# Splitting GpSimd's tensor instructions, and telling the planner of the port that GpSimd shares with VectorE

## The chip, the cores and the metric

The kernel runs on one core of one Trainium2 chip. The metric is the device time of one execution in microseconds (us). The engines are named as in the profile: PE (TensorE, matmul), PEld (its weight loads), DVE (VectorE), ACT (ScalarE), POOL (GpSimd) and SP (SyncE, which only issues DMAs).

## The reference

For each of 8 batches, cosine attention over 12 heads of 448 tokens and 64 channels; its output, laid out as 448 x 768, goes through a two-dimensional Fourier transform whose real part is added, a layer norm and a two-layer FFN with ReLU and a residual:

```python
q_n = q / (norm(q) + 1e-06); k_n = k / (norm(k) + 1e-06)
attn = softmax(q_n @ k_n.T / tau); x = attn @ v          # (8, 12, 448, 64) -> (8, 448, 768)
X = fft(fft(x, axis=1), axis=2); u = x + real(X)
un = (u - mean(u)) / sqrt(var(u) + 1e-06)
out = u + max(un @ w_ch1, 0) @ w_ch2                      # 768 -> 3072 -> 768
```

Inputs and output are float32; the kernel computes its matmuls in bf16.

## The kernel before

The kernel doesn't write out an order by hand. It records about 3,000 operations, each with a list of engines that may do it, an estimated duration, a priority, and what it reads and writes (`Plan.add`, L105). `Plan.schedule` (L143) then plays them through in time: whenever an engine is free it takes, among the operations that are ready first, the one with the lowest priority number. What comes out is one fixed order per engine. `Plan.emit` writes each engine's order with semaphore waits, so on the chip each engine works strictly in that order, and an operation that is late holds back all that is queued behind it on its engine. `SHIFT` (L28) adds constants to the priorities of named operations; it is a table of numbers and decides the order in detail.

Names follow one scheme, a step, its numbers, and the batch: `qk00_2` is a score matmul of batch 2, `sc0_3` a scaling for batch 3. The stages of a batch, and the engines that they use:

- Norms and transposes. For batches 2 to 7 SP loads 128 x 768 pieces of q and k (`ld_`), ACT squares (`sq`), DVE sums (`ss`), ACT and DVE make the reciprocal norm (`ln`, `nrm`, `eps`, `rcp`), POOL multiplies (`sc0` to `sc6`, L722) and SP transposes by DMA (`tr`). For batches 0 and 1 the scalings (`scK`, `scQ`, `scT`) are on DVE and the transposes on PE (`tk`, `tq`).
- Attention. `qk` on PE, `ex` on ACT (exp from PSUM), `pv` on PE, `rd` and `x` on DVE (normalisation), then `fa`, `f`, `g` on DVE, which fold the sequence for the transform.
- Transform. `fs` and `fd` on PE, then `pq`, `u` (residual), `bs`, `ba` (layer-norm statistics), `un` on DVE, and `tru`, a transposing DMA that SP issues and that gives PE its operand.
- FFN. `h` on PE is the first layer, `relu` on ACT or DVE takes it out of PSUM. PSUM has two banks for these products (pool M), so PE stands still when the ReLU two steps back isn't done. For batch 0 the second layer is done directly (`y`). From batch 1 on, two token tiles share seven products `m1` to `m7` in place of eight, which needs sums of hidden blocks (`s1` to `s4`, DVE, L1217) and four sums of weight blocks, `t1` to `t4`, in three parts each (`t10`, `t11`, `t12` and so on; L1276), made once. `t3` overwrites weights that batch 0 still reads, so `t3` and `t4` wait for batch 0's last product. `m6` needs `t2`, `m5` `t1`, `m7` `t3`, `m4` `t4`. Outputs leave PSUM by ACT and get a residual from POOL (`fa0p`, `fv0p`, `fm0p`; L1148), or by DVE (`fin`), and are stored by SP or by an indirect DMA from POOL (`sc_1_0`).

PE has the most work, so the planner fills it: PE's idle places in the plan get filler matmuls (`Plan.fill`, L243), whose results nobody reads. A filler is put in PE's order, waits for the DVE operation that the plan has finished just before it, and writes columns 450 to 512 of a PSUM bank. They keep PE from idling for long; the trace records a TensorE clock that is granted at full or at half rate.

POOL's DMAs (weights `W1_`, `W2_`; values `ld_v`) stand in POOL's order like its arithmetic. The W1 and W2 loads are chained: each waits for the landing of the third before it.

Of the kernel before, what the change touches and what calls it, by code (L numbers as in the profile page):

```python
# [2 lines left out]

# [3 lines left out]
AluOp = mybir.AluOpType  # L7
# [21 lines left out]
    "ix0": {0: 108.5}, "ldt0": {0: 220.8}, "scT0_0": {0: 4.6}, "scK1_0": {0: 211.1}, "ek1_0": {0: 171.4}, "ek2_0": {0: -26.8}, "tq2_0": {0:  # L29
    136.3}, "et0_0": {1: -181.4}, "ld_q1_0": {0: 5.1}, "sqK1_0": {0: 9.2}, "nrm0": {2: -2.9}, "eps0": {2: -104.2}, "ssT1_0": {0: -11.8}, "ln0":  # L30
    {3: -6.1}, "scT3_0": {0: -68.7}, "scK4_0": {0: -50.6}, "scQ4_0": {0: 6.1}, "scT4_0": {0: 72.4}, "scK5_0": {0: 18.9}, "scT5_0": {0: -38.2},
    "ek3_0": {0: 0.7}, "tq3_0": {0: -15.6}, "eq3_0": {0: -21.7}, "et1_0": {1: 112.3}, "half": {1: 331.9}, "ld_v2_0": {0: -9.9}, "pv11_0": {0:
    17.1}, "rd1_0": {0: 250.5}, "qk22_0": {0: -118.5}, "tpd": {0: 74}, "tqd": {0: 221.6}, "u0_0": {3: 2.3}, "u224_0": {0: 25.7}, "u1_0": {2:
    11.1, 4: 7.7}, "eu00_0": {0: -63.8}, "bs1_0": {0: -1.8, 1: -2.6}, "un2_0": {0: -44.8}, "W1_0": {0: 0.013}, "scK0_1": {0: -0.7}, "scT0_1":
    {0: -306.7}, "tq2_1": {0: -24.4}, "ln1": {2: -23.6}, "rcp1": {2: 63.5}, "sqQ1_1": {0: -27.7}, "scK5_1": {0: 644.3}, "scQ5_1": {0: 190.2},
    "ek3_1": {0: -9.4}, "tq4_1": {0: 5.7}, "eq4_1": {0: -135.4}, "tt1_1": {0: -229.4}, "ex0_1": {0: 7.5, 1: -623, 3: 418.3}, "pv00_1": {0: 127},
    "ex1_1": {2: 107.9}, "qk1t_1": {0: 20.1}, "ex3_1": {0: 509.1}, "qk2t_1": {0: 311.3}, "pv20_1": {0: 40.2}, "fa1_1": {1: -84.5}, "relu0_0":
    {0: 13.6}, "relu10_0": {0: 199.5}, "fin01_0": {0: 115.9}, "t40": {0: 144.2}, "t21": {0: 84.1}, "u0_1": {3: -26}, "u1_1": {3: 31.1, 4: 24.3,
    5: 52.7}, "bs0_1": {1: -82.5}, "bs3_1": {0: -0.6}, "sq0_2": {0: -193}, "ln2": {0: 5.2}, "sc1_2": {0: 53.9}, "ld_k0_2": {0: -1.8}, "ss3_2":
    {1: 7}, "eps2": {3: 52.6, 5: 52.6}, "ss5_2": {0: 25.7}, "sq5_2": {1: 343.5}, "ld_k2_2": {0: -6.2}, "ex3_2": {0: 306, 1: 306}, "g0_2": {0:  # L40
    33.7}, "te0_2": {0: 14.9}, "qk4t_2": {0: 250.7}, "x4_2": {0: 3.5}, "g1_2": {0: -470.2}, "s21_1": {0: 252.1}, "fd0_2": {0: 0.2}, "u0_2": {1:
    -300.3}, "pq1_2": {0: 46.9}, "un0_2": {0: 4.2}, "ss0_3": {0: -154.8}, "ss1_3": {1: -75.1}, "tr1_3": {0: 14.7}, "ss2_3": {0: 449.6}, "sq2_3":
    {1: -527.6}, "tr3_3": {0: 56.4}, "ss4_3": {1: -209.3}, "eps3": {4: 98.6}, "sq6_3": {0: 1.2}, "ss6_3": {1: -24.9}, "ex0_3": {3: 2}, "x0_3":
    {0: 41.1}, "ex1_3": {2: 103.4}, "qk20_3": {0: -294.6}, "pv50_3": {0: 69.4}, "rd4_3": {0: -2.5}, "f01_3": {0: 230.6}, "relu22_2": {0: 148.6},
    "fd1_3": {0: 116.4}, "u1_3": {3: 275.9, 4: 212.2}, "bs1_3": {0: 7.8}, "rs1_3": {0: 154.6}, "tr1_4": {0: -3.5}, "ss4_4": {0: -161.2},
    "ld_k2_4": {0: -0.1}, "qk20_4": {0: -3}, "pv20_4": {0: 84.3}, "pv50_4": {0: 78}, "gc1_4": {0: 152.1}, "relu20_3": {0: 11.7}, "s21_3": {0:
    37.2}, "s31_3": {1: 42.1}, "ln5": {2: -325.5}, "pv00_5": {0: 1.4}, "qk1t_5": {0: 2.3}, "qk20_5": {0: -436.1}, "pv30_5": {0: 1.5}, "fa0_5":
    {1: 325.8}, "g0_5": {0: 10.3}, "relu8_4": {1: 56.3}, "fd0_5": {0: 4.5}, "pq0_5": {0: 280.5}, "pq1_5": {1: 218.4}, "sq6_6": {0: 33.9},
    "rcp7": {0: -136.1}
}  # L50


# [3 lines left out]
class Op:  # L56
    __slots__ = ("engs", "eng", "fn", "durs", "prio", "deps", "raw", "start", "end",
                 "idx", "acquire", "uses", "dma", "name", "seq", "margin", "serve", "order")

    def __init__(self, engs, fn, durs, prio, name, serve=0.0, margin=0.0):  # L60
        self.engs = engs
        self.eng = None
        self.fn = fn
        self.durs = durs
        self.serve = serve
        self.prio = prio
        self.deps = set()
        self.order = ()
        self.raw = set()
        self.start = self.end = None  # L70
        self.idx = None
        self.acquire = None
        self.uses = ()
        self.dma = None
        self.name = name
        self.margin = margin

# [10 lines left out]
class Plan:  # L88
# [54 lines left out]
    def schedule(self):  # L143
# [6 lines left out]
        ready = {e: [] for e in self.ENGS}  # L150
        free = {"pe": 1.0, "act": 2.0, "dve": 1.0, "pool": 0.85, "sp": 0.7}
# [35 lines left out]
        while left:  # L187
# [38 lines left out]
            if e == "pool" and op.dma is not None and self.order[e] and self.order[e][-1].dma is None:  # L226
                d += 0.6
            op.start = t
# [14 lines left out]
    def fill(self, t0, t1, after, make, least=0.3):  # L243

        live = {0: [], 1: []}
        for op in self.ops:
            for t in op.acquire or ():
                if t.pool == "M":
                    live[t.slot].append((op.start, max(u.end for u in t.users), t))
        out, t = [], t0  # L250
        for op in self.order["pe"]:
            if op.start > t0 and op.end <= t1 + 1.0 and op.start - t > least:
                bank = [x for x in (0, 1) if not any(a < op.start and b > t for a, b, _ in live[x])]

                for x in range(int((op.start - t) / 0.4)) if bank else ():
                    at = t + 0.4 * x
                    new = Op(("pe",), make(bank[0], 8), (0.288,), 0, "warm")
                    new.eng, new.start, new.end = "pe", at, at + 0.288
                    new.deps.add(after)
                    new.deps.add([o for o in self.order["dve"] if o.end + PE_LAT <= at + 0.1][-1])  # L260
                    new.deps.update(u for a, b, tile in live[bank[0]] if b <= t for u in tile.users[-2:] if u.eng != "pe")
                    out.append(new)
            out.append(op)
            t = max(t, op.end)
# [77 lines left out]
class Kern:  # L342
# [336 lines left out]
    def norm(self, b):  # L679
        P = self.P  # L680
# [17 lines left out]
        for i, (kind, t, dmas) in enumerate(items):  # L698
# [15 lines left out]
            for x in range(ns):  # L714
# [7 lines left out]
            P.add(("pool",), lambda v, i=i, buf=buf, qh=qh: v.tensor_tensor(  # L722
                v3(qh), v3(buf), RN[:, i, :].unsqueeze(2).to_broadcast((128, H, DH)), AluOp.mult),
                (1.5,), pr, f"sc{i}_{b}", reads=bn + [f"RN_{i}t"],
# [415 lines left out]
    def fin(self, b, tile, op, ob, c, ut, src, nm):  # L1140
# [3 lines left out]
        if src == "a":  # L1144
# [3 lines left out]
            self.P.add("pool", lambda g: g.tensor_tensor(self.OUTB[:, ob, cs], self.OUTB[:, ob, cs], self.U[:, ut, cs], AluOp.add), 0.95, -1,  # L1148
                       f"{nm}p_{b}", reads=[on] + self.unames(b, ut), writes=[on])
# [112 lines left out]
    def sums(self, done):  # L1262
# [7 lines left out]
        for k in range(3):  # L1270
            for nm, o, a, bb, rd, wr, af in (
# [4 lines left out]
                P.add(("pool", "dve"), lambda e, o=o, a=a, bb=bb: e.tensor_tensor(o, a, bb, AluOp.subtract), (3.15, 1.8), 190, f"{nm}{k}",  # L1276
                      reads=rd, writes=wr + old * (nm != "t3"), after=af)
# [109 lines left out]
```

## Time and profile before

| | us |
|---|---|
| median of 3 runs | 603.44 (602.99 to 607.24) |
| the profiled execution | 601.36 |
| its span, first to last instruction | 599.5 |
| before the first FFN matmul (`h0_0`) | 52.7 |
| end of batch 0's last product | 122.7 |
| first FFN matmul of batch 1 (`h0_1`) | 130.05 |

The profile records one execution; its own time, 601.36 us, is 1.9 us above its span and 2.1 us below the median of the three runs. In its rows a group has a line of the kernel, an engine, an operation, what it writes and reads, and a count; then busy time, the mean duration of one, and the idle time before them with what ended it. The planner's names above are put to the trace's instructions by their place in each engine's order. In a timeline row the first number is the start from the span's beginning, the second the length.

### The profile page before, as it was taken

Reading aid. Unit: us, or ns where it says so; the run is one execution under the profiler, and the core shown is the slowest. Engines: PE = TensorE matmul, PEld = TensorE weight load, DVE = VectorE, ACT = ScalarE, POOL = GpSimd, SP = SyncE. Lnnn points to the kernel's source line nnn. Section 1 sums busy time; section 2 is a strip of 40 time slices with the busy share of each in tenths; the row PEclk is TensorE's granted clock in tenths of the full one; section 3 lists DMA queues with packets and bytes.
Section 4 is the critical chain, followed back from the end, with each engine's and each line's share of the span. In section 5 each row is a group of like instructions: output and inputs, shape, how many; then the busy total and the mean of one; then the engine's idle time right before and its main releaser. Section 6 shows DMA issues by size and latency. Waiting matters only on the chain.

```text
span 599.5 us, 15228 instructions
## 1 busy us (share of the span) xinstructions
PE 572.9 (96%) x6298; PEld 445.5 (74%) x6298; DVE 431.0 (72%) x969; ACT 353.6 (59%) x678; POOL 212.0 (35%) x214
## 2 busy tenths in 40 slices
PE   4888999988999999999999999999999999999997
PEld 4568786666778578678778678668878778678684
DVE  6868887899789868985768767986888477711313
ACT  7885796435876886348766786458536644224140
POOL 8843344568244144331270426222340120200302
PEclk9889999979999999999999999999999999999999
DMA  9999999945179459354299149654492010210001
GB/s 215 126 203 222 177 196 144 170 103 109 28 150 148 68 147 111 81 121 107 55 136 162 42 130 111 110 121 119 62 104 56 15 54 2 67 40 27 27 27 53
DMA packets 187637, 62.13 MB, mean 104 GB/s; under 512 B 166704, under 2 KB 185392, under 8 KB 187568
## 3 DMA queue, kind: packets, MB, share of 16 engines
q1 hardware_dynamic: 129648, 38.35, 33.2%
q0 software_dynamic: 57920, 22.81, 29.6%
q8 instruction: 49, 0.80, 0.6%
q14 instruction: 20, 0.16, 0.1%
HBM read 51.90 MB, written 11.01 MB: 105 GB/s over the span
## 4 chain that ended last, share of the span: by engine, by line
PE 82%; DVE 7%; POOL 5%; ACT 2%; DMA 2%; issue 2%; POOLq 0%; DVEq 0%
PE PS L1095 35%; PE PS L1126 30%; PE PS L838 5%; PE PS L801 4%; PE PS L925 2%; PE PS L963 2%; DVE U L991 2%; PE PS L832 2%; DMA W1b<-in_moe_w_ch_dram 1%; POOL TX L1276 1%; DVE ACG L1020 1%; DVE HQ L1217 1%; DMA W2b<-in_moe_w_ch_dram 1%; PE PS L813 1%; POOL W1b L512 1%
## 5 line engine op out<-in xcount | busy, mean ns | idle before, releaser
L1095 PE MATMUL PS<-UNT,W1b 128*128 128x256 bf16 (+1 forms) x2304 | 236.1, 260 | 3.5 <-DVE HQ L1111 2.5
L1095 PEld LDWEIGHTS PS<-UNT,W1b 128*128 128x128 bf16 x2304 | 199.0, 98 | 28.0 <-issue 3.2
L781 ACT ACTIVATE E<-PS 128x900 bf16<-128x900 f32 (+1 forms) x192 | 147.8, 829 | 27.8 <-PE PS L801 24.5
L1126 PE MATMUL PS<-W2b,HQ 128*128 128x384 bf16 x768 | 133.9, 326 | 0.0
L1111 ACT ACTIVATE HQ<-PS 128x512 bf16<-128x512 f32 x117 | 69.9, 597 | 92.1 <-PE PS L1095 91.5
L1126 PEld LDWEIGHTS PS<-W2b,HQ 128*128 128x128 bf16 x768 | 73.6, 98 | 46.6 <-issue 2.0
L1217 DVE TENSOR_TENSOR HQ<-HQ 128x512 bf16<-128x512 bf16 x141 | 70.2, 522 | 43.0 <-ACT HQ L1111 30.2
L722 POOL TENSOR_TENSOR QH<-STG,SM 128x768 bf16<-128x768 f32 x42 | 62.9, 1498 | 74.6 <-DVE SM L535 46.6
L1148 POOL TENSOR_TENSOR OUTB<-OUTB,U 128x384 f32<-128x384 f32 x33 | 32.0, 969 | 157.0 <-ACT OUTB L1146 156.7
L1126 PE MATMUL PS<-TX,HQ 128*128 128x384 bf16 x396 | 71.3, 326 | 0.0
L1126 PEld LDWEIGHTS PS<-TX,HQ 128*128 128x128 bf16 x396 | 37.7, 98 | 24.1 <-issue 1.3
L838 PE MATMUL PS<-VB,E 128*128 128x65 bf16 x1152 | 52.5, 195 | 0.0
L838 PEld LDWEIGHTS PS<-VB,E 128*128 128x128 bf16 x1152 | 49.0, 99 | 1.5
L715 ACT ACTIVATE QH<-STG 128x384 f32<-128x384 f32 x84 | 42.3, 523 | 13.1 <-DVE SM L717 9.8
L1111 DVE TENSOR_SCALAR HQ<-PS 128x512 bf16<-128x512 f32 x45 | 31.1, 690 | 26.0 <-PE PS L1095 25.7
L717 DVE TENSOR_REDUCE SM<-QH 128x6 f32<-128x384 f32 x84 | 43.7, 541 | 6.6 <-ACT QH L715 6.4
L1176 POOL DMA_INDIRECT out_dram<-OUTB,IDX x20 | 21.0, 1050 | 76.6 <-DVE OUTB L1154 43.8
L832 PE MATMUL PS<-VZ,E 128*128 128x130 bf16 x192 | 41.9, 221 | 2.1 <-DVE X L858 1.8
L801 PE MATMUL PS<-QT,KT 64*128 64x225 bf16 x576 | 40.2, 260 | 2.3 <-DVE SM L534 1.4
L991 DVE TENSOR_TENSOR U<-ACG,X 128x384 bf16<-128x384 f32 (+3 forms) x70 | 40.8, 611 | 0.8
L761 POOL DMA_DIRECT2D VB<-in_v_dram x24 | 25.6, 1073 | 27.2 <-PE PS L838 24.6
L801 PEld LDWEIGHTS PS<-QT,KT 64*128 64x128 bf16 x576 | 22.5, 94 | 17.1 <-issue 4.6
(135 smaller groups left out, 649.5 us busy)
## 6 DMA issues: line engine op xcount, KB each, us to landing
STG<-in_k_dram SPq DMA_DIRECT2D x18, 384.0 KB, 3.7
STG<-in_q_dram SPq DMA_DIRECT2D x18, 384.0 KB, 4.5
VB<-in_v_dram POOLq DMA_DIRECT2D x24, 192.0 KB, 7.5
W1b<-in_moe_w_ch_dram POOLq DMA_DIRECT2D x12, 384.0 KB, 7.7
W2b<-in_moe_w_ch_dram POOLq DMA_DIRECT2D x12, 384.0 KB, 6.5
out_dram<-OUTB SPq DMA_DIRECT2D x7, 384.0 KB
TX<-in_k_dram SPq DMA_DIRECT2D x2, 576.0 KB, 5.5
TX<-in_q_dram SPq DMA_DIRECT2D x2, 576.0 KB, 6.0
```

Of the source, the lines that this page charges most:

```text
L715: P.add("act", lambda a, sq=sq, src=buf[:, w * x:w * x + w]: a.activation(sq, src, ACTF.Square), t_act(w), pr, f"sq{i}_{b}", reads=bn, wri ...
L717: P.add("dve", lambda v, o=SS[:, i, H // ns * x:H // ns * (x + 1)], sq=sq: v.tensor_reduce(o, sq.rearrange("p (h d) -> p h d", d=DH), AX.X ...
L722: P.add(("pool",), lambda v, i=i, buf=buf, qh=qh: v.tensor_tensor(v3(qh), v3(buf), RN[:, i, :].unsqueeze(2).to_broadcast((128, H, DH)), Al ...
L781: return a.activation(o, self.PS[:, bk:bk + nc_, 0:SQ2], ACTF.Exp, scale=1.0 / self.tau)
L801: i = pe.matmul(self.PS[:, bk + h, c0:c0 + NK], self.KT[r, jj, kt * 128:(kt + 1) * 128], self.QT[r, jj, cols], start=True, stop=True)
L832: r = pe.matmul(o, st(6), self.VZ[:, j, :], start=not split, stop=(split and i == 0), skip_group_check=True)
L838: r = pe.matmul(o[:, 65 * h:65 * h + 65], st(2 * kt + h), self.VB[:, kt, 2 * j + h, :], start=(split and i == h == kt == 0), stop=((not sp ...
L991: return v.tensor_tensor(U[o0:o0 + n, ut, cs].rearrange("p (i e) -> p i e", e=2), src, X[i0:i0 + n, x, cs].rearrange("p (i e) -> p i e", e ...
L1095: r = pe.matmul(self.PS[:, bk, x * n:(x + 1) * n], self.W1b[:, j, ft * 128:(ft + 1) * 128], self.UNT[:, j, cs], start=(j == 0), stop=(j == ...
L1111: return e.activation(o, i, ACTF.Relu) if e is self.nc.scalar else e.tensor_relu(o, i)
L1126: r = pe.matmul(self.PS[:, bk, 0:n], lhs(f), rhs(f), start=(start and f == 0), stop=(stop and f == NF // 2 - 1), skip_group_check=True)
L1217: P.add("dve", lambda v: v.tensor_tensor(cs(o), cs(a), cs(bq), op), 0.46, -0.5, f"{nm}{k}_{b}", reads=rd, writes=hr(o)(k))
```

## The change

Four things are changed.

1. GpSimd's `tensor_tensor` instructions are split. The scaling `sc` of 12 heads becomes three instructions of 4 heads, the residual add of 384 columns becomes two of 192, and a weight sum of 4 x 384 columns becomes four of 384. The weight sums, which the planner could put on POOL or on DVE, are now on POOL alone. Their planned durations go from 1.5, 0.95 and 3.15 to 1.7, 1.05 and 3.4 us.
2. The planner knows the piece length of these operations (`PIECE`) and a list of DVE operations (`PORT`). A DVE operation of the list that would start while such a POOL operation runs is planned to start at the end of the piece that runs then.
3. A filler may use any of five PSUM banks (before: the two of pool M) and consists of 11 matmuls in place of 8.
4. `SHIFT` is replaced as a whole by another table.

```diff
+PIECE = {r"sc\d_\d": 0.57, r"f[avm]\dp_\d": 0.52, r"t\d\d": 0.85}
+PORT = r"eps\d|f[a01]\d_\d|g\d_\d|u\d+_\d|un\d_\d|s\d\d_\d|sc[KQT]\d_\d"
...
+        self.piece = next((x for n, x in PIECE.items() if re.fullmatch(n, name)), 0.0)
+        self.port = re.fullmatch(PORT, name) is not None
...
+            if e == "pool" and op.piece:
+                port.append((t, t + d, op.piece))
+            elif e == "dve" and op.port and port and port[-1][1] > t:
+                x, y, z = port[-1]
+                d += x + z * math.ceil((t - x + 0.02) / z) - t
...
-        live = {0: [], 1: []}
+        live = {x: [] for x in (0, 1, 2, 4, 6)}
...
-                bank = [x for x in (0, 1) if not any(a < op.start and b > t for a, b, _ in live[x])]
+                bank = [x for x in live if not any(a < op.start and b > t for a, b, _ in live[x])]
...
-                    new = Op(("pe",), make(bank[0], 8), (0.288,), 0, "warm")
+                    new = Op(("pe",), make(bank[0], 11), (0.34,), 0, "warm")
...
-            P.add(("pool",), lambda v, i=i, buf=buf, qh=qh: v.tensor_tensor(
-                v3(qh), v3(buf), RN[:, i, :].unsqueeze(2).to_broadcast((128, H, DH)), AluOp.mult),
-                (1.5,), pr, f"sc{i}_{b}", reads=bn + [f"RN_{i}t"],
+            def scale(v, i=i, buf=buf, qh=qh):
+                for h in range(0, H, 4):
+                    r = v.tensor_tensor(v3(qh)[:, h:h + 4], v3(buf)[:, h:h + 4], RN[:, i, h:h + 4].unsqueeze(2).to_broadcast((128, 4, DH)), AluOp.mult)
+                return r
+            P.add("pool", scale, 1.7, pr, f"sc{i}_{b}", reads=bn + [f"RN_{i}t"],
...
-            self.P.add("pool", lambda g: g.tensor_tensor(self.OUTB[:, ob, cs], self.OUTB[:, ob, cs], self.U[:, ut, cs], AluOp.add), 0.95, -1,
+            def plus(g):
+                for x in range(cs.start, cs.stop, 192):
+                    xs = slice(x, x + 192)
+                    r = g.tensor_tensor(self.OUTB[:, ob, xs], self.OUTB[:, ob, xs], self.U[:, ut, xs], AluOp.add)
+                return r
+            self.P.add("pool", plus, 1.05, -1, f"{nm}p_{b}", reads=[on] + self.unames(b, ut), writes=[on])
...
-                P.add(("pool", "dve"), lambda e, o=o, a=a, bb=bb: e.tensor_tensor(o, a, bb, AluOp.subtract), (3.15, 1.8), 190, f"{nm}{k}",
+                def fn(e, o=o, a=a, bb=bb):
+                    for x in range(4):
+                        r = e.tensor_tensor(o[:, x], a[:, x], bb[:, x], AluOp.subtract)
+                    return r
+                P.add("pool", fn, 3.4, 190, f"{nm}{k}", reads=rd, writes=wr + old * (nm != "t3"), after=af)
```

## The prediction

> **What bounds the kernel now.** The page comes first. PE is busy nearly everywhere; what is missing lies at the start and in the ninth and tenth slices, where the granted clock dips too.
>
> ```profile
> PE 572.9 (96%) x6298; PEld 445.5 (74%) x6298; DVE 431.0 (72%) x969; ACT 353.6 (59%) x678; POOL 212.0 (35%) x214
> PE   4888999988999999999999999999999999999997
> PEclk9889999979999999999999999999999999999999
> PE 82%; DVE 7%; POOL 5%; ACT 2%; DMA 2%; issue 2%; POOLq 0%; DVEq 0%
> ```
>
> So I priced PE by its matmuls' starts. From `h0_0` (52.73 us) to the last matmul (596.3) at the trace's own spacings (109 ns for 256 columns, 162 for 384) the work is 513.9 us and the fillers 2.7; 26.9 us are lost, of which 11.2 are about 0.013 us at each of 890 steps, which no reordering removes. The rest, 15.7, is all that there is to win behind `h0_0`: 6.5 around the start of batch 1's FFN with its fillers, 2.6 at one ReLU, 2.2 near 400 us, some 4 between 66 and 97.
>
> The timelines of three engines at batch 1's start show the cause:
>
> ```profile
> 122.97 3.31 POOL L1276 TENSOR_TENSOR W2b<-W2b 128x1536 bf16<-128x1536 bf16 x1 [5.32 <-PE PS L1126]
> 123.83 3.44 DVE L991 TENSOR_TENSOR U<-ACG,X 32x384 bf16<-32x384 f32 x2
> 126.75 3.49 PE L1326 MATMUL PS<-W1b 128*128 128x62 bf16 x64 [2.49 <-DVE U L991]
> 130.05 1.25 PE L1095 MATMUL PS<-UNT,W1b 128*128 128x256 bf16 x5
> ```
>
> Two residual adds take 0.55 us each; the first took 2.86, until 0.41 us after `t30` had ended on POOL. PE's fillers wait for that add, and `h0_1` stands behind them, though its operand (`tru1_1`) had landed at 126.11. The same again inside the layer:
>
> ```profile
> 142.69 4.37 DVE L1217 TENSOR_TENSOR HQ<-HQ 128x512 bf16<-128x512 bf16 x2 [0.47 <-ACT HQ L1111]
> 143.69 3.08 POOL L1276 TENSOR_TENSOR TX<-W2b 128x1536 bf16<-128x1536 bf16 x1
> 147.71 0.83 PE L1095 MATMUL PS<-UNT,W1b 128*128 128x256 bf16 x6 [2.47 <-DVE HQ L1111]
> ```
>
> `s31_1` waits for `t12`, a ReLU stands behind it, and PE behind the ReLU. Summed over all DVE instructions that overlap POOL arithmetic, against the median of those that don't (0.42 us for `s`, 0.55 for `u`), the excess is about 31 us, 14.5 of it on 25 of the 141 `s`. Most is hidden: from 160 to 560 us PE stands still only near 400.
>
> **POOL: split.** Durations before, from the groups of all lines:
>
> ```profile
> L722 POOL TENSOR_TENSOR QH<-STG,SM 128x768 bf16<-128x768 f32 x42 | 62.9, 1498 | 74.6 <-DVE SM L535 46.6
> L1148 POOL TENSOR_TENSOR OUTB<-OUTB,U 128x384 f32<-128x384 f32 x33 | 32.0, 969 | 157.0 <-ACT OUTB L1146 156.7
> L482 POOL TENSOR_TENSOR U<-U,UNT 128x192 f32<-128x192 f32 (+1 forms) x4 | 2.3, 593 | 0.1
> L1276 POOL TENSOR_TENSOR TX<-W2b 128x1536 bf16<-128x1536 bf16 x2 | 6.2, 3090 | 0.2
> L1276 DVE TENSOR_TENSOR TX<-W2b,TX 128x1536 bf16<-128x1536 bf16 x3 | 4.6, 1537 | 0.0
> ```
>
> Undisturbed, a scaling takes 1.47, an add 0.91, a weight sum 3.09. The split adds 42x2 + 33 + 12x3, and five sums come over from DVE: 158 instructions (210 to 368). A further instruction costs at least the 0.06 us that POOL's rows show between neighbours, and at most 0.28 (two of 192 columns take 2x0.593, one of 384 takes 0.91). I take 0.11, which the change's own durations also imply (3.40 against 3.09 in three extra pieces); so 3.42 a sum, 1.69 a scaling. DVE loses five sums (7.7 us in this trace). Elsewhere the 17 us of added POOL time lie beside PE: POOL is busy 35%.
>
> [...]
>
> **DVE beside POOL.** [...]
>
> ```profile
> 94.53 1.47 POOL L722 TENSOR_TENSOR QH<-STG,SM 128x768 bf16<-128x768 f32 x1 [0.17 <-POOL QH L722]
> 96.17 1.50 POOL L722 TENSOR_TENSOR QH<-STG,SM 128x768 bf16<-128x768 f32 x1 [0.17 <-POOL QH L722]
> 95.91 2.04 DVE L875 TENSOR_TENSOR ACG<-X 128x512 bf16<-128x512 bf16 x2
> ```
>
> The first `fa` slips in at 96.0, the second waits out the whole scaling. I assume that the same happens between pieces, so a DVE step waits at most a piece (0.8 us in place of 3.1). In return each such step holds up POOL's next piece: 0.03 to 0.62 us in nine places of the trace; I take 0.25, bounds 0 and 0.41.
>
> **Batch 1's start, step by step**, from the end of batch 0's last product (Y, 122.7 before). The changed program puts `fin21`, `ba`, `ba`, one `u`, `un0`, `un1` on DVE behind Y, beside `t40` (before, `un0` and `un1` were done by Y+0.6). `fin21` and the two `ba` end at Y+0.95; then `u`, `un0`, `un1` each wait for a piece: 2.1, 3.05, 4.0. `tru0` and `tru1` issue in 1.25 us each, the second lands 1.5 us later: Y+7.1. PE's order has 5 fillers, `qk00_2`, 15 fillers, `h0_1`; the last two fillers wait for the second `ss6_2`, seven DVE steps behind `un1`: Y+7.5, so `h0_1` starts at Y+8.3 (before 7.35). `qk00_2` (0.56 us of work) is now in the gap; the half-clock stretch that cost `h0_1` to `h12_1` 1.2 us I take as gone, since more fillers run; the ReLU stall of 2.6 I take as gone too.
>
> New is a queue on POOL. All ten weight sums left at Y are on it. To the end of `t22`, which the third part of `m6` needs: 8 sums x 3.42 = 27.4, 4 scalings x 1.69 = 6.8, a scatter with its wait 1.9, 12 gaps of 0.13 = 1.6, 14 DVE turns x 0.25 = 3.5: Y+41.2. PE, at the trace's start-to-start times, is there 28.0 us after `h0_1`, at Y+36.3. `fa0p` stands behind `t22` (1.2), `fin00` (0.55) behind that, and `m50` needs the bank that `fin00` frees: Y+43.1 in place of Y+37.0. From there 9.98 us to the third part of `m4`: Y+53.1, against 174.08 = Y+51.4 before: **+1.7**. Bounds: 0.06 a piece and no DVE turns make t22 Y+36, which gives -3.4; 0.28 and 0.41 give Y+49, +9.2.
>
> **Before that.** DVE's `sinn` waited for POOL's second `half`, queued behind a W1 load:
>
> ```profile
> 35.29 0.40 DVE L745 TENSOR_SCALAR HQ<-CS 128x900 bf16<-128x900 bf16 x1 [3.22 <-POOL CS L742]
> ```
>
> PE lost 1.97 at `pv50`, ACT 2.5 before its next exp. Now `half` follows the third W1 issue, near 20.6 us by the rows' durations, and `sinn` meets it. Next late is the table chain on POOL, whose last `tad` ends near 33.6 (31.5 before), and `tmd`, queued on DVE ahead of `rd3`. The exps end near 38.5 in place of 39.98; a third `u` ahead of the first `bs` costs 0.46, `eu01` on ACT behind `eu00` 0.2: `h0_0` **-0.8** (-2 to +1). In batch 0 the transposes stand between `h` steps where now 3 us are lost, but `y001` still meets the last W2 load, issued behind `t20`, which is longer: **-0.5** (-2 to +2). Near 400 us ACT's `ln22` stood ahead of an exp and waited for a DVE chain that POOL had delayed: **-1.8** (-2.2 to 0). Fillers on other banks cost nothing there: both plans have none behind `h0_1`. Later batches: 0, as their DVE waits are hidden already (0 to +3 if the new order makes some).
>
> **Sum:** -0.8 - 0.5 + 1.7 - 1.8 = -1.4 us on 601.36, so 600.0; the median of the runs is 2.1 higher: **602.0**.
>
> **Rivals.** (1) POOL keeps up: pieces near 0.06 us and cheap DVE turns, -3.4 in place of +1.7: 597. For it: 0.05 to 0.09 us between POOL's dependent neighbours. Against it: the 192-column row. (2) POOL falls behind: 0.28 a piece and a DVE turn at most boundaries; it decides from a `t22` later than Y+44, and at Y+49 gives +9.2 - 3.1 = +6.1: 610. For it: five sums moved to a POOL that is full for 40 us. Against it: DVE has only 14 such steps there. (3) The split doesn't do what it says: back-to-back pieces of one operation leave no gap (the rows above had 0.17), so DVE still waits out 3.4 us; then `h0_1` is at Y+14.5, POOL's chain ends no later, and ReLU stalls stay, 4 us over the forecast: 606. [...] No row here has such a pair with DVE waiting.
>
> **Chances.** Forecast 0.48, (1) 0.25, (2) 0.17, (3) 0.10. 1% (6 us) is about what a measurement of this kernel can tell from no change. Two thirds of (1) and a little of the forecast lie below 597.4: 0.22 faster; (2) and some of (3) above 609.5: 0.20 slower; 0.58 within. The range takes in (1) with its share of the other gains and (2): 594 to 610.
>
> **What would show it.** `u`, `un` and `s` at Y to Y+45 at most 1.3 us long; no PE wait of 2.5 us on an add or a ReLU; `h0_1` near Y+8; PE waiting for POOL's L1276 or for `fa0p` around Y+37 to Y+43; L722 pieces near 0.56, L1276 pieces near 0.85. The forecast is wrong if a weight sum takes under 3.3 or over 3.8 us, or if stalls appear in batches 2 to 7 that the old order hadn't.

## The result

The changed kernel is slower by a little: 608.22 us median of 20 runs (600.0 to 609.24), the kernel before 603.57 beside it; the ratio is **1.0053, 95% interval 1.003 to 1.0077**. The ratios of this document leave out the runs of a slower state, so they are not the quotients of the medians. The forecast had said 602.0, 1.4 us under the kernel before, with 594 to 610 as its range. The profiled execution took 607.41 us, its span is 605.6 (before 601.36 and 599.5). Nineteen of the twenty times lie between 606.2 and 609.2 and one lies at 600.0, to which the account below comes back.

These lines of the page after answer to those shown of before: busy times, PE's slices and granted clock, the chain that ended last, POOL's two split groups, and the two groups that turn out to carry the result.

```profile
PE 577.9 (95%) x6554; PEld 450.3 (74%) x6554; DVE 424.2 (70%) x969; ACT 351.0 (58%) x673; POOL 255.1 (42%) x372
PE   5899969999879999999999999999999999999997
PEclk9999998999989999999999999999999999999999
PE 77%; POOL 11%; DMA 8%; issue 2%; DVE 1%; SPq 0%; ACT 0%; POOLq 0%; ACTq 0%
L739 POOL TENSOR_TENSOR QH<-STG,SM 128x256 bf16<-128x256 f32 x126 | 78.2, 648 | 69.2 <-DVE SM L550 48.6
L1168 POOL TENSOR_TENSOR OUTB<-OUTB,U 128x192 f32<-128x192 f32 x66 | 37.6, 590 | 139.9 <-ACT OUTB L1163 138.7
L730 ACT ACTIVATE QH<-STG 128x384 f32<-128x384 f32 x84 | 42.4, 520 | 23.1 <-DMA STG<-in_k_dram 11.8
L818 PE MATMUL PS<-QT,KT 64*128 64x225 bf16 x576 | 40.4, 262 | 9.0 <-ACT QH L730 6.5
```

DVE's share of the chain has gone from 7% to 1%, which fits what was meant: its waits for POOL are off the path. POOL's share has gone from 5% to 11%, DMA's from 2% to 8%. PE's slices now dip at the sixth and at the eleventh and twelfth place, the clock right behind them. The last two rows name the sixth: ACT's squares (L730) waited 11.8 us for loads of k, and score matmuls waited 6.5 us for those squares. Cut at the forecast's own points, the two profiled executions compare so:

| stretch | before | after | change | forecast |
|---|---|---|---|---|
| start to `h0_0` | 52.73 | 50.57 | -2.2 | -0.8 |
| `h0_0` to the end of batch 0's last product (Y) | 69.97 | 77.53 | **+7.6** | **-0.5** |
| Y to `h0_1` | 7.35 | 8.42 | +1.1 | +0.95 |
| `h0_1` to the third part of `m4` | 44.03 | 46.10 | +2.1 | +0.8 |
| from there to the end of the span | 425.4 | 423.0 | -2.4 | -1.8 |

Four rows came out within 1.4 us of the forecast. The second is 8.1 us off, more than the whole error of 7.5. The first row is not as exact as it looks: in seven further profiled executions, of kernels below with the same order up to there, `h0_0` started between 50.27 and 52.39.

**Where the 7.6 us are.** The timelines of PE, ACT and SP in the changed kernel (start, length, engine, line; in brackets the idle time before and what ended it):

```profile
83.78 1.36 PE L1112 MATMUL PS<-UNT,W1b 128*128 128x256 bf16 x11
91.64 0.94 PE L818 MATMUL PS<-QT,KT 64*128 64x225 bf16 x8 [6.50 <-ACT QH L730]
92.51 4.30 PE L1112 MATMUL PS<-UNT,W1b 128*128 128x256 bf16 x24
82.02 0.90 ACT L798 ACTIVATE E<-PS 128x900 bf16<-128x900 f32 x1
89.79 0.94 ACT L730 ACTIVATE QH<-STG 128x384 f32<-128x384 f32 x2 [6.87 <-DMA STG<-in_k_dram]
90.63 0.53 ACT L798 ACTIVATE E<-PS 128x450 bf16<-128x450 f32 x1
76.83 0.59 SPq L721 DMA_DIRECT2D STG<-in_q_dram  x1
77.47 2.03 SPq L721 DMA_DIRECT2D STG<-in_k_dram  x2
```

ACT stands from 82.93 to 89.79 on `sq2_2`, the first square of batch 2's k rows, whose load SP issued at about 79. Behind it in ACT's order is the exp `ex3_1` (90.63) that frees the PSUM slot of `qk50_1`, and behind the sum of squares on DVE stand `x2_1` and a ReLU. So PE stops at 84.98 (the start of its last matmul and the 0.11 us that each takes; the row's modelled end is 85.14) and starts again at 91.64. The waits of PE below are counted in this way, 0.16 us longer than in the rows. The 24 `h` matmuls after it take 4.30 us in place of 2.6, while the granted clock is at one half from 88.8 to 95.6: some 2 us more.

What had changed around that load stands in the timelines, of SP and POOL in the kernel before and of POOL in the changed one:

```profile
78.18 0.37 SPq L706 DMA_DIRECT2D STG<-in_k_dram  x1
82.98 2.11 POOL L513 DMA_DIRECT2D W2b<-in_moe_w_ch_dram  x3 [7.81 <-DVE KTD L676]
```

```profile
78.76 2.11 POOL L528 DMA_DIRECT2D W2b<-in_moe_w_ch_dram  x3 [5.25 <-DVE QH L632]
```

These are `W2_8` to `W2_10`. By the recorded plan they wait for DVE's last scaling of batch 1, `scK5_1`, and are issued 0.4 us behind it in both traces (the brackets name what DVE finished about then). Before, that ended at 82.56, and the k load, issued at 78.2, had landed by 82.6. The new order has `scK5_1` done at 78.35; the three W2 loads then go out just as batch 2's three loads do, and the k load lands at 89.7. The DMA engines were as full before (1.28, 1.26 and 1.15 in the stretches 80 to 83, 83 to 86 and 86 to 89), but by then the k load was there, and ACT worked on.

### The profile page after: what moved, and what is told of

The parts are those of the page before. It is cut to its first block, busy times and chain, and to the rows that moved or that the text cites. A ratio compares the mean times of both kernels' runs of the same rounds, so it can differ in the third digit from the quotient of the medians.

```text
span 605.6 us, 15899 instructions
## 1 busy us (share of the span) xinstructions
PE 577.9 (95%) x6554; PEld 450.3 (74%) x6554; DVE 424.2 (70%) x969; ACT 351.0 (58%) x673; POOL 255.1 (42%) x372
## 4 chain that ended last, share of the span: by engine, by line
PE 77%; POOL 11%; DMA 8%; issue 2%; DVE 1%; SPq 0%; ACT 0%; POOLq 0%; ACTq 0%
PE PS L1143 32%; PE PS L1112 31%; PE PS L855 4%; PE PS L818 4%; POOL TX L1299 4%; DMA W1b<-in_moe_w_ch_dram 4%; DMA W2b<-in_moe_w_ch_dram 2%; PE PS L942 2%; DMA STG<-in_k_dram 2%; PE PS L980 2%; PE PS L849 1%; POOL W2b L1299 1%; POOL QH L739 1%; POOL W1b L527 1%; POOL VB L778 1%
## 5 line engine op out<-in xcount | busy, mean ns | idle before, releaser
L1128 ACT ACTIVATE HQ<-PS 128x512 bf16<-128x512 f32 x113 | 67.5, 597 | 95.9 <-PE PS L1112 95.6
L739 POOL TENSOR_TENSOR QH<-STG,SM 128x256 bf16<-128x256 f32 x126 | 78.2, 648 | 69.2 <-DVE SM L550 48.6
L1238 DVE TENSOR_TENSOR HQ<-HQ 128x512 bf16<-128x512 bf16 x141 | 67.7, 502 | 42.8 <-ACT HQ L1128 29.4
L1168 POOL TENSOR_TENSOR OUTB<-OUTB,U 128x192 f32<-128x192 f32 x66 | 37.6, 590 | 139.9 <-ACT OUTB L1163 138.7
L730 ACT ACTIVATE QH<-STG 128x384 f32<-128x384 f32 x84 | 42.4, 520 | 23.1 <-DMA STG<-in_k_dram 11.8
L1128 DVE TENSOR_SCALAR HQ<-PS 128x512 bf16<-128x512 f32 x49 | 33.8, 690 | 28.7 <-PE PS L1112 27.6
L855 PE MATMUL PS<-VB,E 128*128 128x65 bf16 x1152 | 51.0, 193 | 0.1
L855 PEld LDWEIGHTS PS<-VB,E 128*128 128x128 bf16 x1152 | 47.5, 97 | 1.4 <-issue 0.2
```

The costliest lines, as they stand in the source:

```text
L730: P.add("act", lambda a, sq=sq, src=buf[:, w * x:w * x + w]: a.activation(sq, src, ACTF.Square), t_act(w), pr, f"sq{i}_{b}", reads=bn, wri ...
L739: r = v.tensor_tensor(v3(qh)[:, h:h + 4], v3(buf)[:, h:h + 4], RN[:, i, h:h + 4].unsqueeze(2).to_broadcast((128, 4, DH)), AluOp.mult)
L855: r = pe.matmul(o[:, 65 * h:65 * h + 65], st(2 * kt + h), self.VB[:, kt, 2 * j + h, :], start=(split and i == h == kt == 0), stop=((not sp ...
L1128: return e.activation(o, i, ACTF.Relu) if e is self.nc.scalar else e.tensor_relu(o, i)
L1238: P.add("dve", lambda v: v.tensor_tensor(cs(o), cs(a), cs(bq), op), 0.46, -0.5, f"{nm}{k}_{b}", reads=rd, writes=hr(o)(k))
```

## The experiments

Theory **A**: six transfers of 0.39 MB share the DMA engines, so batch 2's loads are late. Rival **B**: the k load is late only because it has become the second on SP's queue. Rival **C**: the load's time is harmless; what hurts is which steps stand behind it. Apart from the load, a second suspect is the POOL queue near 169 us, and a third question is what the pieces, the fillers and the order are worth singly. Moves are made after planning, so everything else of the plan stays: `behind(x, y)` takes step `x` out of its engine's order and puts it right behind `y`, on `y`'s engine. The edits are shown as calls of it, with comments added and the rest left out.

```diff
         self.P.fill(first, self.est, self.id_op, warm(self.W1b[:, 0, 0:128]), 1.2)
...
+        def behind(x, y):
+            x, y = at[x], at[y]              # by name and occurrence
+            self.P.order[x.eng].remove(x)
+            x.eng = y.eng
+            o = self.P.order[y.eng]
+            o.insert(o.index(y) + 1, x)
...
         self.P.emit(self.nc, self.es)
```

### SP's order as before

```diff
+        behind("ld_t3_2#0", "ld_k0_2#0")
```

> The changed kernel with one step moved: on SP's queue the load of batch 2's k rows (ld_k0_2) goes ahead of that of the tail rows (ld_t3_2), as it did before the change; ACT's and POOL's orders stay. In the changed kernel ACT stood from 82.93 to 89.79 us on ld_k0_2, and PE 6.66 us at qk50_1 behind it, with a half-clock stretch after it that cost some 2 us. Theory A (the loads are slow because three W2 loads share the DMA engines with them from 78.8 on): the k load lands near 81, but the tail load, which ACT's sq0_2 needs first, now lands near 85, so ACT stands there some 3.4 us instead, PE waits about 3 us at qk50_1, and 3 to 5 us are gained: 603 to 605. Theory B (only the place on SP's queue counts; the first load is quick, the second late): the tail load takes the wait over, lands near 89, and the time stays at 607 to 609. Theory C (the loads were ready and the wait is for something else): no change of any wait.

Measured: 608.86 us, ratio to the kernel before 1.0083 (1.0038 to 1.0128): nothing gained. The k load landed at 84.08, but the tail load, now second, at 89.50 and the q load at 94.70, 5 us apart each. ACT's squares in 70 to 100 us:

```profile
L730 ACT ACTIVATE QH<-STG 128x384 f32<-128x384 f32 x6 | 2.9, 516 | 7.7 <-DMA STG<-in_k_dram 5.1 <-DMA STG<-in_q_dram 2.6
```

The wait is about as long as it was, on other transfers (the tail load holds q rows and k rows). PE lost 4.16 us at `qk3t_1`. B's time came true and A's did not: A had put the second load at 85. The wait only moved to the load that is now second, and the one behind it was late too; the next runs decide.

### Two of the three W2 loads later

```diff
+        behind("W2_9#0", "t10#0")
+        behind("W2_10#0", "W2_9#0")
```

> The changed kernel with two W2 loads (W2_9, W2_10) issued behind the weight sum t10 on POOL, some 4 us later (near 83.6), while SP, ACT and DVE keep their orders; W2_11 is issued when it was. Theory A (shared DMA engines): only W2_8 then runs beside the tail and k loads, three transfers of 0.39 MB at some 0.2 MB/us, so the k load lands near 84.6 in place of 89.7; ACT's wait falls from 6.9 to some 1.7 us, PE's at qk50_1 from 6.66 to some 1.5, the half clock behind it goes, and the time is 600 to 602. Theory B (the place on SP's queue): the k load still lands near 89, PE still waits over 5 us, 607 to 609.

Measured: 603.12 us, ratio 0.9978 (0.9938 to 1.0018), 5 us less than the changed kernel. SP's order is the bad one, yet the k load landed at 86.45 and the q load at 87.64; ACT waited 3.2 us and PE 2.94 at `qk50_1`. That is A in kind, with a load 1.9 us later, a wait twice as long and a time a microsecond above its range; B, which had left the load at 89, falls. The half clock stayed (from 89.6 to 93.0).

### All three W2 loads later

```diff
+        behind("W2_8#0", "t10#0")
+        behind("W2_9#0", "W2_8#0")
+        behind("W2_10#0", "W2_9#0")
```

> The changed kernel with three W2 loads (W2_8 to W2_10) issued behind the weight sum t10 on POOL, near 84 us, so that no W2 load is issued while batch 2's three loads are under way. Theory A (the stall is a matter of six transfers of 0.39 MB sharing the DMA engines at some 0.2 MB/us; which of the three is late only decides where PE stands): the k load lands near 83 and the q load near 85, ACT's waits for loads between 80 and 95 come to under 1 us together, PE at qk50_1 waits under 1 us. W2_11 then lands near 96, PE wants it near 95: 1 to 1.5 us. 600 to 602. Theory B (what matters is the place on SP's queue): as much lost as with only two W2 loads moved, 603.

Measured: 601.38 us, ratio 0.9958 (0.9935 to 0.998). POOL's timeline, and the stretches 80 to 92 us of this kernel (window: its length, ACT's busy time and count, granted clock, DMA share, GB/s):

```profile
81.34 3.52 POOL L1299 TENSOR_TENSOR TX<-W2b 128x384 bf16<-128x384 bf16 x4 [8.43 <-PE PS L681]
85.56 2.17 POOL L528 DMA_DIRECT2D W2b<-in_moe_w_ch_dram  x3 [0.69 <-DVE SM L732]
80.00:83.00 3.00, 2.90 (x5) 1.00 1.05 212
83.00:86.00 3.00, 2.65 (x6) 1.00 0.40 78
86.00:89.00 3.00, 2.48 (x6) 1.00 0.66 92
89.00:92.00 3.00, 2.36 (x8) 1.00 1.12 193
```

The same stretches of the changed kernel:

```profile
80.00:83.00 3.00, 2.48 (x4) 1.00 1.06 176
83.00:86.00 3.00, 0.00 (x0) 1.00 1.18 222
86.00:89.00 3.00, 0.00 (x0) 0.97 1.16 203
89.00:92.00 3.00, 2.21 (x5) 0.50 1.08 179
```

In the changed kernel the DMA engines are full for twelve microseconds (shares of 1.06 to 1.18) at about 0.2 MB/us, and ACT does nothing for six of them. With the W2 loads behind, they have room from 83 to 89 (0.40 and 0.66), ACT waits for no load at all, PE doesn't stop there, and the granted clock stays at 1.00. PE then waits 1.79 us for `W2_11`, as expected within 0.3. That settles A against B: SP's order here is the changed kernel's.

How the loads shared the DMA engines shows in the profile's count of packets. Packets, MB and share of the DMA engines' time by queue (q0 carries POOL's loads, q1 SP's), from 85 to 88 us in the changed kernel, then from 80 to 84 us with the W2 loads behind:

```profile
q0 software_dynamic: 353, 0.52, 94.4%
q1 hardware_dynamic: 352, 0.09, 22.1%
```

```profile
q1 hardware_dynamic: 3330, 0.84, 105.1%
```

From 85 to 88 us in the changed kernel the two queues moved as many packets (353 and 352), but a packet of W2 has 1536 B and one of SP's loads 256 B. So SP's loads got 0.03 of the 0.2 MB/us there, and 0.21 in the second stretch, alone: what A's transfers shared evenly in that stretch were packets, not bytes. SP's loads landed 5.4 and 5.2 us apart beside the W2 loads (84.08, 89.50 and 94.70, in the run with SP's order as before) and 1.6 apart without them (85.98 and 87.53, in the kernel with both repairs below).

### The exps ahead of the squares

```diff
+        # ACT: ex3_1, ex5_1 twice, and only then the squares
+        behind("sq2_2#0", "ex5_1#1"); behind("sq0_2#1", "sq2_2#0")
+        behind("sq1_2#0", "sq0_2#1"); behind("sq2_2#1", "sq1_2#0")
+        # DVE: x2_1 and three ReLUs, and only then the sums of squares
+        behind("ss2_2#0", "relu20_0#1"); behind("ss0_2#1", "ss2_2#0")
+        behind("ss2_2#1", "ss0_2#1"); behind("ss1_2#0", "ss2_2#1")
```

> The changed kernel with the transfers left as they are, but what waits for the k load taken out of the way: on ACT ex3_1, ex5_1 (twice) go ahead of sq2_2, sq0_2, sq1_2, sq2_2, and on DVE x2_1 and three ReLUs ahead of the sums of squares ss2_2, ss0_2, ss2_2, ss1_2. Theory (the only price of the late load is what stands behind it in ACT's and DVE's orders): the k load still lands near 89.7, but PE reaches qk50_1 with no wait over 0.5 us and no half clock follows; end of batch 0's last product near 120 in place of 128.1, 599 to 600 in all. Rival (PE would be held at the next step by something as late, the last W2 load at 93.5 or batch 2's own norms): half of it comes back, 603 to 605.

Measured: 606.86 us, ratio 1.0047 (1.0009 to 1.0084): no better than the changed kernel within the intervals, and worse than either expectation. `qk50_1` waited no more, but the stall came back at `qk5t_1`, from 91 us on:

```profile
92.20 0.94 ACT L730 ACTIVATE QH<-STG 128x384 f32<-128x384 f32 x2 [3.21 <-DMA STG<-in_q_dram]
95.96 0.27 PE L830 MATMUL PS<-QT,KTD 128*128 128x225 bf16 x1 [4.92 <-ACT E L798]
```

In this run the k load landed at 85.96, the q load at 92.18; ACT stood on the next square with the next exps behind it. So moving the steps behind the load didn't help by itself here: with the loads still late, another square stood in front of an exp. Over the five kernels whose three W2 loads went out before the last of batch 2's loads, PE lost 4.2 to 6.7 us between 84 and 97 us, at places that changed from one to the next.

### The POOL queue shortened

The forecast had put a queue on POOL at `t22` and `fa0p`, and there it is. POOL and PE of the changed kernel:

```profile
165.05 3.88 POOL L1299 TENSOR_TENSOR TX<-W2b,TX 128x384 bf16<-128x384 bf16 x4 [0.17 <-POOL QH L739]
169.06 1.05 POOL L1168 TENSOR_TENSOR OUTB<-OUTB,U 128x192 f32<-128x192 f32 x2
169.07 0.81 PE L1143 MATMUL PS<-TX,HQ 128*128 128x384 bf16 x4 [2.15 <-POOL TX L1299]
170.77 1.46 PE L1143 MATMUL PS<-TX,HQ 128*128 128x384 bf16 x4 [0.89 <-DVE OUTB L1175]
```

`t22` ends at Y+40.8 and the third part of `m6` waits for it; `fa0p` follows, then `fin00`, then `m50` at Y+42.7. The last row takes 1.46 us for four matmuls: the granted clock is at one half again, from 170.74 to 174.15. The repair gives two sums back to DVE where it stood idle:

```diff
+        behind("t31#0", "s30_1#0"); behind("t21#0", "t31#0")   # to DVE
+        behind("t22#0", "t12#0")                               # ahead of sc2_3
+        behind("fin00_1#0", "s42_1#0")
```

> The changed kernel with POOL's queue after batch 0's last product (Y) made shorter: the weight sums t21 and t31 go to DVE, behind s30_1, where it stood idle 3.6 us; t22 goes ahead of the scaling sc2_3 on POOL; and fin00_1 goes on DVE behind the last s step. The stall on the loads of batch 2 stays. My forecast said that the queue to t22 and fa0p costs the path some 6 us at m60 and m50 (measured in the changed kernel: 2.32 + 1.05 + 0.30 + 0.23, and 1.75 of half clock). If so: t22 ends near Y+32, no wait over 0.5 us at m60 or m50, no half clock there, 5 us less: 602 to 604. Rival (the two sums on DVE hold up the ReLUs behind them, 2 us at h10_1 or h20_1, and PE then meets the next late step): 605 to 608.

Measured: 601.18 us, ratio 0.9941 (0.9908 to 0.9973), 7 us less than the changed kernel where 5 were expected. `t22` ended at 160.90 (Y+31.4), and `m6` and `m5` run through, in 2.76 us for 16 matmuls:

```profile
165.11 2.76 PE L1143 MATMUL PS<-TX,HQ 128*128 128x384 bf16 x16
```

The stall of the loads was still there (1.73 us at `qk50_1`, 4.39 at `h22_0`). A stall of 1.81 us at `qk22_2` near 157 went as well, which nobody had counted and which would account for most of the 2 us.

### Both repairs

```diff
+        behind("W2_8#0", "t10#0"); behind("W2_9#0", "W2_8#0"); behind("W2_10#0", "W2_9#0")
+        behind("t31#0", "s30_1#0"); behind("t21#0", "t31#0")
+        behind("t22#0", "t12#0"); behind("fin00_1#0", "s42_1#0")
```

> The changed kernel with both: W2_8 to W2_10 behind t10, and t21 and t31 on DVE, t22 ahead of sc2_3, fin00_1 ahead. If the two stalls are separate and add up (6 to 7 us and some 5): 595 to 598, faster than both kernels. Rival (once PE is ahead it meets batch 2's norm chain, which follows the loads and not PE): only half of it, 600 to 602.

Measured: **595.59 us, ratio 0.9841 (0.979 to 0.9892)**: faster than both kernels, and the two gains add up: against the changed kernel's ratio of 1.0053 they are 0.95 and 1.12 points alone and 2.12 together, some 13 us. (Each ratio was measured beside the kernel before, on different chips.) The stretches around batch 0's end and the start of batch 1, in the changed kernel and then with both repairs (length, busy time and count of PE, PEld, DVE, ACT, POOL; clock; DMA share; GB/s):

```profile
150.00:180.00 30.00, 25.31 (x256) 16.51 (x254) 22.95 (x41) 18.54 (x34) 28.46 (x36) 0.94 0.25 61
80.00:100.00 20.00, 13.50 (x129) 9.99 (x129) 9.46 (x22) 9.84 (x21) 10.63 (x15) 0.83 0.73 127
```

```profile
150.00:180.00 30.00, 29.89 (x325) 21.59 (x324) 26.68 (x55) 20.38 (x39) 26.55 (x34) 1.00 0.50 92
80.00:100.00 20.00, 19.98 (x266) 15.43 (x264) 15.80 (x36) 15.21 (x29) 15.21 (x21) 1.00 0.93 165
```

PE goes from 13.50 to 19.98 us of twenty and from 25.31 to 29.89 of thirty, at full clock in both.

### The pieces joined again, with and without the repairs

```diff
-                for h in range(0, H, 4):            # sc: three pieces
+                for h in range(0, H, 12):           # one
...
-                for x in range(cs.start, cs.stop, 192):
+                for x in range(cs.start, cs.stop, 384):
...
-                    for x in range(4):
-                        r = e.tensor_tensor(o[:, x], a[:, x], bb[:, x], AluOp.subtract)
+                    r = e.tensor_tensor(o, a, bb, AluOp.subtract)
```

(with the slices widened to match)

> The changed kernel's orders with the POOL instructions joined again: scalings in one instruction, adds in one of 384 columns, weight sums in one of 1536. My forecast's rival (3) said what this would give: behind the last product of batch 0 (Y) the third u, un0 and un1 would each wait out a whole weight sum on DVE (2.9 us and more in place of 1.2, 1.0, 1.1), h0_1 would start at Y+14.5 in place of Y+8.4, ReLUs behind s steps would wait again, and the end of t22 would come some 4 us earlier against Y, so that the stall at m60 and m50 goes: net +2 to +6, 610 to 614. Rival (the pieces buy nothing, since DVE gets in at the end of a sum either way): h0_1 within 1 us of Y+8.4, POOL ends earlier, and the time falls to 603 to 606. The wait for the k load of batch 2 near 83 stays in both.

> The kernel with both repairs and POOL's instructions joined again (scalings, adds and weight sums in one instruction each). With the changed kernel's orders the joined form cost 12 us against the pieces: h0_1 at Y+15.1 in place of Y+8.4, a ReLU stall of 3.7 us at h10_1, 2.6 us at qk5t_2. Two sums fewer on POOL leave t40, t30 and t11 beside un0 and un1 as they were. If the pieces are what gets DVE's short adds through: h0_1 again near Y+15, 603 to 608, so 8 to 12 us worse than with pieces. Rival (the loss was POOL's long queue, which two sums fewer have shortened): 597 to 600.

Measured: 620.46 us, ratio 1.0263 (1.0191 to 1.0334), and with the repairs 609.84, ratio 1.011 (1.0033 to 1.0187). Against the same orders with pieces that is some 12 and 14 us more by the medians, 2.1 and 2.7 points by the ratios; both times lie above either expectation. DVE behind Y, first in the changed kernel, then in its joined form:

```profile
129.37 1.19 DVE L1008 TENSOR_TENSOR U<-ACG,X 32x384 bf16<-32x384 f32 x1
130.59 1.95 DVE L1046 TENSOR_SCALAR F<-U,MV 128x768 bf16<-128x768 bf16 x2
```

```profile
131.29 2.34 DVE L1008 TENSOR_TENSOR U<-ACG,X 32x384 bf16<-32x384 f32 x1
133.67 6.29 DVE L1046 TENSOR_SCALAR F<-U,MV 128x768 bf16<-128x768 bf16 x2
133.29 3.28 POOL L1298 TENSOR_TENSOR W2b<-W2b 128x1536 bf16<-128x1536 bf16 x1
```

With pieces, `un0` and `un1` take 0.96 and 1.07 us, joined 3.12 and 3.24; they end at 136.79 and 139.96, 0.2 us after two of the weight sums. `h0_1` starts at Y+15.3 (15.1 with the repairs) in place of Y+8.4, a ReLU stall of 3.7 us is back at `h10_1`, and 2.6 us at `qk5t_2` (2.1 with the repairs). POOL's sums are shorter, but its chain did not end earlier: `t22` ended at Y+45.8, because the scaling ahead of it (`sc2_3`, at 170.96) waited for a reciprocal norm that DVE brought late (170.73). So in this order the pieces are worth more than the forecast's rival (3) had said.

### The pieces alone, in the old order

The kernel before, with the loops of pieces above and its planner, durations and `SHIFT` kept, so that the orders are the old ones and DVE keeps its five weight sums.

> The kernel before, its planner, durations and step priorities kept (so its orders are the same), with POOL's scalings in three pieces, adds in two and weight sums on POOL in four. It says whether the pieces or the new order made the changed kernel slower. If the pieces alone are a gain: the u add behind batch 0's last product takes 1.2 us in place of 2.86, the ReLU at h10_1 no longer waits 2.5 us, the stall near 400 us goes, the half clock at h0_1 with the first; POOL's sums are 0.4 us longer each, beside other work: 595 to 598. Rival (without a plan for the longer POOL steps, t12 and t32 or the scalings come late for PE): 602 to 606.

Measured: 601.28 us, ratio 0.9965 (0.9921 to 1.0008): a little faster or the same, between the two expectations. `h0_1` came at Y+6.5 in place of Y+7.35 and the ReLU stall at `h10_1` fell from 2.6 to 1.7 us. But with the longer `t10` and `t20` `W2_11` landed at 98.44 (`y001` waited 1.35 us for it, before 0.73), the wait for `sinn` in the start stayed with the old order, and of the one near 400 us half stayed (0.89 at `qk0t_6`, before 1.66). The pieces alone don't make the kernel slower; the order that came with them does, and, repaired, makes it faster.

### The fillers

Both on top of the two repairs: the old rule (banks 0 and 1, 8 matmuls), and none behind the first `h0_0`.

```diff
-        live = {x: [] for x in (0, 1, 2, 4, 6)}
+        live = {0: [], 1: []}
...
-                    new = Op(("pe",), make(bank[0], 11), (0.34,), 0, "warm")
+                    new = Op(("pe",), make(bank[0], 8), (0.288,), 0, "warm")
```

> The kernel with both repairs (W2 loads behind t10; two sums on DVE) and the old rule for fillers: only PSUM banks 0 and 1, 8 matmuls of 62 columns each. Both rules put 20 fillers into the gap ahead of batch 1's first h0, 160 matmuls in place of 220. Theory (the new banks and the longer fillers cost and bring nothing behind the first h0_0): 595 to 597, as with the new rule. Rival (the longer fillers hold the clock up and the shorter ones do not): half clock at h0_1 to h12_1, 1 to 1.5 us more, 597 to 598.

> The kernel with both repairs and no filler matmuls behind the first h0_0 (the 20 fillers between batch 0's last product and h0_1 are left out). PE then stands idle for some 1.5 us, does qk00_2, and stands idle for 6 us more. In the changed kernel idle stretches of 2.3, 2.9 and 6.7 us were followed by a half clock from some 4 us after their start, for 3.4 to 6.8 us. Theory: h0_1 starts where it did (Y+8.3 to 8.5, tru1_1 sets it), its first 3 to 6 us run at half clock, 1.5 to 2.5 us more than with fillers: 597 to 598.5. Rival (the fillers themselves hold h0_1 up through their waits on DVE): h0_1 starts earlier than Y+8 and the time stays at 595 to 596.5.

Measured, on one chip: 593.59 us, ratio 0.9835 (0.9762 to 0.9907), with the old rule, and 594.96, ratio 0.9857 (0.9782 to 0.9931), with none. The old rule is as good as the new one (0.9841 above). Without fillers PE stood idle from 122.39, and the clock was at one half from about 126.6 to 133.4:

```profile
126.00:127.00 1.00, 0.00 (x0) 0.78 0.62 119
130.00:131.00 1.00, 1.00 (x7) 0.50 0.98 185
133.00:134.00 1.00, 1.00 (x10) 0.80 0.00 0
```

The first four `h` took 4.5 us from start to start in place of 2.6, while `h0_1` came 0.4 us sooner (Y+7.73 against 8.13 with the old rule). Net 1.5 us by the rows, 1.4 by the medians. The old rule came 1.4 us under its range. Of the two expectations for leaving the fillers out both had a part: with fillers of either rule the granted clock was 1.00 all the way from 122 to 138, and `h0_1` came 0.4 us later.

## Why the forecast was wrong

**The step that failed** is "Before that. ... In batch 0 ...: -0.5 (-2 to +2)". It measured +7.6. The step looked at PE's order, at the one W2 load that PE waits for (`y001`, `W2_11`), and at POOL's longer `t20`. It did not follow the other W2 loads to what they run beside. DVE's new order freed `W2_8` to `W2_10` 4.2 us earlier; that looks like a gain. Here it took the bandwidth of three loads that ACT had queued squares for, ahead of an exp that PE needed: 6.66 us of wait and some 2 of half clock. The other profiled executions bear this out: from `h0_0` to Y the five kernels that kept the three W2 loads early took 75.9 to 78.2 us, the one with two of them moved 74.4, the five with all three moved 69.3 to 71.4, and the kernel before 70.0. Each link was open to view in the trace of before and in the planned orders: loads and W2 loads at 0.2 MB/us when alone and in packets of 256 and 1536 B, SP's loads gated on `W2_7`, `sq2_2` ahead of `ex3_1`. The rivals had no such case either, nor had the signs named for being wrong; the one rival that ended slower was POOL's queue. Its 610 alone widened the range to take in 608, and its mechanism did not come: that is luck. That the one run at 600.0 us was one without this wait is possible, but no trace shows it.

**Start:** right in kind. The wait of `sinn` went, and `h0_0` came 2.16 us earlier where -0.8 was taken and -2 was the bound. Over the eight profiled executions with this order it came 0.3 to 2.5 us earlier than in the one of before, 1.2 on average, so part of the 2.16 belongs to this execution. The table chain on POOL, taken as next late, ended at 32.15 where 33.6 was taken.

**Batch 1's start:** right, step by step. `u`, `un0`, `un1` each waited for a piece (1.19, 0.96, 1.07 us), `h0_1` came at Y+8.42 (8.3), and the last fillers waited for the second `ss6_2` (135.73), which ended as `tru1_1` landed (135.71). No half clock there (1.00 from 126 to 150), no ReLU stall at `h10_1`.

**POOL's queue:** right in place and time. `t22` ended at Y+40.8 (41.2), `m50` started at Y+42.7 (43.1). Mis-sized was what follows: behind the waits of 2.3 and 1.05 us came a half clock (170.74 to 174.15) that the sum did not have, so the third part of `m4` came at Y+54.5 in place of Y+53.1. A sum on its own took 3.51 us, not 3.42, so a further piece costs 0.14 us and not 0.11; the scalings (1.75 against 1.47) and the adds (1.05 against 0.91) give the same 0.14. The lower bound of 0.06 us is not borne out. DVE's turns took 0 to 0.5 us from each sum (3.51 to 4.01), in keeping with the 0.25 a turn that was taken. With them five of the eight sums up to `t22` lasted over 3.8 us, which the forecast had named as a sign of being wrong, and yet `t22` came on time: the sign left out the turns that the sum counted.

**Near 400 us:** the stall went (-2.0 by PE's spacings between 400 and 420; -1.8 taken).

**The rivals.** (1) and (2) did not come: `t22` lies between their two bounds. (3), that back-to-back pieces leave no gap, is refuted where it had been open: beside pieces `un0` and `un1` took 0.96 and 1.07 us, beside joined sums 3.12 and 3.24, so DVE got in between pieces. Its `h0_1` was near (Y+14.5 said, 15.3 and 15.1 in the joined forms); its total of 4 us was a third of the 12 and 14 that joining cost.

Without the 8.1 us of that step the changed kernel would take some 600 us, an estimate from 608.2; the kernel with the W2 loads moved back measured 601.4, with 1.8 us of it a new wait for `W2_11`.

## What to carry to other kernels

When an engine's steps come earlier, write down what each of them releases, the DMAs first, and what is under way on the same DMA engines at that time; here the W2 loads that went out sooner were paid for by the loads beside them, whose packets of 256 B got 0.03 of the 0.2 MB/us beside packets of 1536 B. A step that waits for a DMA should not stand ahead of one that the busiest engine needs soon, but moving such steps brought next to nothing here while the transfers stayed late: repair the cause, then the order. Cutting POOL's long instructions let DVE through sooner here (0.96 and 1.07 us in place of 3.12 and 3.24 for `un0` and `un1`) and cost 0.14 us a piece; count the pieces into POOL's queue where PE waits for its end.

## What was new about the hardware

- **Two DMA queues at work together moved as many packets each, not as many bytes.** In the changed kernel W2's queue and SP's moved 353 and 352 packets from 85 to 88 us, of 1536 and of 256 B, and in each half microsecond of that stretch the two counts lie within three of each other (59 and 60 in the first, 55 and 52 in the last). The stream of small packets so got a seventh of the bytes (0.09 of 0.61 MB). Where W2's queue moved only 7 packets, from 83.5 to 84.0, SP's moved 477.
- **Some stops of PE were followed by a halved clock, also after PE was at work again, and how a stop lay in time seems to decide.** In the run with two W2 loads moved, PE stopped at 85.6, worked again from 88.4, and the granted clock fell at 89.6 and rose at 93.0. In the traces of the kernel before and of the changed kernel all falls and rises lie whole multiples of 3.41 us apart, up to the program's end: in the changed kernel the falls at 88.82 and 170.74 are 24 of them apart, and a half-clock stretch lasts one or two (170.74 to 174.15, 88.82 to 95.65). When these two traces are cut into pieces of 3.41 us at those times, from 40 to 560 us, the pieces at full clock that a half clock followed have 3.41 and 2.60 us of idle PE in the changed kernel and 1.82 in the kernel before; of the others none has over 1.50. So the stops at `m6` and `m5` fell into one piece in the changed kernel (2.60 us of idle), and the half clock behind it cost 1.7 us more, while the kernel before had a stop of 2.47 us, from 145.24 to 147.71, that fell into two pieces (1.19 and 1.28) and left the clock at 1.00. A stall of PE should be priced with that.
- **Which transfer was late was not stable.** With the same orders on SP and POOL up to there, the k load landed at 89.7 in the changed kernel, at 85.96 with the exps ahead and near 87.0 with POOL's queue shortened; in the last two the q load came at 92.18 and 93.55 and held ACT instead.
